# Two hT tiles, a new split of PSUM for batch 0 and a newly searched order in an attention-then-MoE kernel

## The chip, the cores and the metric

One core of a Trainium2 chip. A time is the device time of one execution in microseconds (us); what is compared are medians of several executions and ratios of fast runs. A run counts as slow when it is over 1.5% above the fastest run of the same kernel; with one core there is no second die to compare with. The profile is of one execution, and its span, from the first to the last instruction, is some 1.6 us shorter than that execution's time.

## The reference

Eight batches. In each, eight heads of 576 rows and 64 columns go through a linear attention (k^T v, then q times that), a norm over the 64 columns, and then as one sequence of 576 rows of 512 through one expert, chosen for the whole batch by the mean of its rows.

```python
def _attn_ref(q, k, v, g_norm):                       # (8, 8, 576, 64)
    kv = np.einsum('bhsd,bhse->bhde', k, v)
    out = np.einsum('bhsd,bhde->bhse', q, kv)
    rms = np.sqrt(np.mean(out * out, axis=-1, keepdims=True) + 1e-06)
    return out / rms * g_norm

def _moe_ref(x, w_gate, w1, w2):                      # x (8, 576, 512), w1 (8, 512, 1024), w2 (8, 1024, 512)
    logits = x.mean(axis=1) @ w_gate
    e_idx = np.argmax(logits, axis=1)
    ...                                               # gate_w: softmax probability of the chosen expert
    h = np.maximum(x[mask] @ w1[e], 0.0)
    out[mask] = gate_w[mask, None, None] * (h @ w2[e])
```

With the inputs the batches choose experts 4, 4, 7, 6, 5, 1, 3, 1. So batch 1 needs no new weights (batch 0 has them), and batch 7 has those of batch 5.

## The kernel before

The kernel is written as small steps, and one string gives the order in which all of them are emitted. Each engine's program then has its own instructions in that order. A token is batch, step, index, and an x where the step's copy or eviction goes to the other of VectorE and ScalarE. The steps that matter here:

- L0, L1, L2: load q, k or v of a batch (GpSimd issues it, 576 KB each; the load casts f32 to f16).
- T, K, O, M, X: transposes of q; k^T v; q times it; the mean of squares (ones times the squares); the normed xT.
- G0 to G3: the gate; G1 reads the chosen expert into a register.
- W0, W1: fetch the expert's first and second weights ("W1 of batch b" is bW0, "W2 of batch b" is bW1; 1024 KB each as f16).
- m0 to m7: the eight units of mm1 (x times W1, into hT); m8 and m9 to m16: mm2 (hT times W2).
- D: dummy matmuls that keep TensorE busy; P: batch 0's own PSUM tiles are given back.

## Time and profile before

| | before |
|---|---|
| time, median of 3 runs | 195.28 us (195.17 to 196.23) |
| span of the profiled run | 191.9 us |
| first matmul of mm1 starts | 30.84 us |
| TensorE idle from 40 to 160 us | 1.65 us |
| last eviction starts, then the end | 187.49 us, 4.4 us |

The main readings (busy shares, slices, windows, chain) are shown in the prediction below.

The timeline of TensorE ahead of mm1 (start us, us, engine, line, operation, out and in, shapes):

```profile
24.59 1.90 PE L149 MATMUL ps_a<-kvb,ones 128*128 128x512 f16 x7
...
26.74 0.95 PE L192 MATMUL ps_a<-vt,kt 96*64 96x64 f16 x48
...
30.84 2.06 PE L348 MATMUL ps_m<-xT,W 128*128 128x288 f16 x8
```

Seven dummies of 512 columns take 1.90 us, 271 ns each; K of batch 1 takes 0.95 us.

### The profile page before, as it was taken

The page shows a single profiled execution, that of the slowest core. Times are in us where ns is not written, and L with a number is a line of the kernel's source. Part 1 is how long each engine was busy: PE and PEld are TensorE (multiplying, and loading weights), DVE is VectorE, ACT ScalarE, POOL GpSimd, SP SyncE. Part 2 cuts the span into 40 slices and gives each one's busy share as a digit, 9 for nine tenths or more (in the row PEclk, how much of TensorE's full clock was granted, in tenths as well). Part 3 has the DMA queues.
Part 4 walks back from the last instruction along what each step waited for, and adds up shares of the span by engine and source line. Part 5 has one row for each costly group of instructions (what it writes and reads, how often), then busy time and mean ns, then how long its engine had stood idle before and what let it go on. Part 6 is the DMA issues. An engine that isn't in the chain of part 4 may idle for free.

```text
span 191.9 us, 4365 instructions
## 1 busy us (share of the span) xinstructions
PE 172.1 (90%) x1691; PEld 113.8 (59%) x1691; DVE 111.2 (58%) x289; ACT 106.6 (56%) x168; POOL 49.9 (26%) x64
## 2 busy tenths in 40 slices
PE   0296687998999999999999999999999999999990
PEld 0153255784668755886478746857686568457540
DVE  2437373867979695775666785697665482431010
ACT  2146105676878757876666656665357656216521
POOL 7770098008223150016117030311022103000000
PEclk9999997999999999999999999999999999999999
DMA  5999999999999999999999999999999898162044
GB/s 157 187 201 206 201 199 186 205 205 204 218 236 246 218 208 215 256 242 204 212 262 236 205 219 243 262 194 177 243 255 181 150 171 195 29 164 59 0 130 116
DMA packets 37031, 36.92 MB, mean 192 GB/s; under 512 B 2706, under 2 KB 30354, under 8 KB 37010
## 3 DMA queue, kind: packets, MB, share of 16 engines
q0 software_dynamic: 29328, 26.30, 86.4%
q1 hardware_dynamic: 7474, 10.05, 18.3%
q10 hardware_dynamic: 208, 0.29, 0.5%
q8 instruction: 13, 0.21, 0.4%
q14 instruction: 8, 0.07, 0.1%
HBM read 61.88 MB, written 9.44 MB: 372 GB/s over the span
## 4 chain that ended last, share of the span: by engine, by line
PE 71%; DMA 16%; DVE 5%; ACT 3%; issue 2%; POOL 2%; POOLq 0%
PE ps_m L348 32%; PE ps_m L387 25%; DMA qt<-in_q_dram 7%; DMA W<-in_moe_w_dram 5%; PE ps_a L224 4%; DMA kt<-in_k_dram 4%; PE ps_a L207 3%; PE ps_a L160 3%; PE ps_m L375 3%; DVE o L179 2%; ACT sq L212 2%; PE ps_a L192 2%; DVE qr L174 1%; POOL qt L103 1%; DVE W L311 1%
## 5 line engine op out<-in xcount | busy, mean ns | idle before, releaser
L348 PE MATMUL ps_m<-xT,W 128*128 128x288 f16 x512 | 69.5, 289 | 0.1
L387 PE MATMUL ps_m<-W,hT 128*128 128x512 f16 x256 | 60.7, 379 | 0.2 <-DMA W<-in_moe_w_dram 0.2
L348 PEld LDWEIGHTS <-W 128*128 128x128 f16 x512 | 50.0, 99 | 13.3 <-issue 0.2
L355 ACT ACTIVATE hT<-ps_m 128x576 f16<-128x576 f32 x51 | 33.2, 652 | 21.0 <-PE ps_m L348 20.7
L387 PEld LDWEIGHTS <-hT 128*128 128x128 f16 x256 | 24.2, 98 | 24.8 <-DMA W<-in_moe_w_dram 0.8
L322 POOL DMA_DIRECT2D W<-in_moe_w_dram x20 | 12.5, 627 | 74.3 <-DVE W L311 23.6
L359 ACT ACTIVATE ot<-ps_m,gates 128x512 f32<-128x512 f32 (+1 forms) x26 | 17.0, 656 | 18.5 <-PE ps_m L387 12.2
L228 ACT ACTIVATE rs<-ps_a,epsc 128x576 f32<-128x576 f32 x28 | 20.5, 741 | 7.5 <-PE ps_a L224 7.0
L237 DVE SCALAR_TENSOR_TENSOR xT<-o,gcol,rs 128x576 f16<-128x576 f32 x28 | 22.4, 812 | 3.6 <-ACT rs L228 3.6
L212 ACT ACTIVATE sq<-ps_a 128x576 f16<-128x576 f32 x28 | 17.9, 648 | 10.9 <-PE ps_a L207 10.8
L179 DVE COPY o<-ps_a 128x576 f32<-128x576 f32 x20 | 15.0, 757 | 14.0 <-ACT sq L212 13.8
L275 POOL TENSOR_TENSOR lg<-base,dl 128x8 f32<-128x8 f32 x8 | 14.2, 1771 | 29.3 <-DVE src L294 16.8
L311 DVE COPY W<-W 128x2048 f16 (+1 forms) x28 | 19.3, 696 | 2.6 <-DVE src L294 0.8
L361 DVE TENSOR_SCALAR ot<-ps_m,gates 128x512 f32<-128x512 f32 (+1 forms) x14 | 9.4, 674 | 17.8 <-PE ps_m L387 15.9
L179 ACT COPY qT<-ps_a 128x576 f16<-128x576 f16 x15 | 9.5, 636 | 10.7 <-PE ps_a L160 10.7
L352 DVE TENSOR_SCALAR hT<-ps_m 128x576 f16<-128x576 f32 x13 | 9.8, 755 | 8.1 <-PE ps_m L348 8.1
L192 PEld LDWEIGHTS <-kt 96*64 96x64 f16 x384 | 7.5, 116 | 9.9 <-ACT kt L179 6.0
L224 PE MATMUL ps_a<-sq,ones 128*128 128x288 f16 x56 | 11.1, 286 | 2.1 <-DVE o L179 2.0
L207 PE MATMUL ps_a<-qT,kvb 128*128 128x288 f16 x56 | 11.6, 291 | 0.8 <-DVE o L179 0.5
L224 PEld LDWEIGHTS <-ones 128*128 128x128 f16 x64 | 6.0, 99 | 7.9 <-issue 3.2
L160 PEld LDWEIGHTS <-qr 96*128 96x128 f16 x144 | 8.9, 100 | 2.9 <-issue 0.4
L160 PE MATMUL ps_a<-ident,qr 96*128 96x96 f16 x144 | 10.4, 209 | 0.2 <-DVE dl L269 0.2
(75 smaller groups left out, 135.1 us busy)
## 6 DMA issues: line engine op xcount, KB each, us to landing
W<-in_moe_w_dram POOLq DMA_DIRECT2D x14, 1024.0 KB, 14.2
out_dram<-ot SPq DMA_DIRECT2D x24, 192.0 KB, 5.8
qt<-in_q_dram POOLq DMA_DIRECT2D x7, 576.0 KB, 14.4
kt<-in_k_dram POOLq DMA_DIRECT2D x7, 576.0 KB, 10.0
vt<-in_v_dram POOLq DMA_DIRECT2D x7, 576.0 KB, 16.1
out_dram<-ot SPq DMA_DIRECT2D x40, 64.0 KB, 5.6
out_dram<-ot SPq DMA_DIRECT2D x16, 128.0 KB, 5.2
W<-in_moe_w_dram POOLq DMA_DIRECT2D x4, 256.0 KB
```

What stands on the lines that cost most here:

```text
L160: nc.tensor.transpose(pt[:, 0, j * R:(j + 1) * R], s["qr"][0:R, c, j], ident[0:R, 0:R])
L179: nc.scalar.copy(out, in_) if x else nc.vector.tensor_copy(out, in_)
L207: nc.tensor.matmul(po[:, i, 0:HS], kvb[:, b % 2, c, :], s["qT"][:, c, i * HS:(i + 1) * HS], start=True, stop=True)
L212: nc.scalar.activation(part(s["sq", c], h), po, AF.Square)
L224: nc.tensor.matmul(pm[:, i if h is None else 0, 0:HS], ones, s["sq", c][:, i * HS:(i + 1) * HS], start=True, stop=True)
L228: nc.scalar.activation(part(s["rs", c], h), pm[:, 0:2 if h is None else 1, 0:HS], AF.Abs_reciprocal_sqrt, bias=epsc)
L237: nc.vector.scalar_tensor_tensor(out=part(s["xT"][:, c, :], h), in0=s["o", c, h], scalar=gcol, in1=part(s["rs", c], h), op0=ALU.mult, op1= ...
L311: nc.vector.tensor_copy(W[:, own, h * n:(h + 1) * n], W[:, ds(sv, 1), h * n:(h + 1) * n].rearrange("p o c f -> p (o c) f"))
L348: nc.tensor.matmul(ph[:, i, 0:HS], w1[:, c, fb * P:(fb + 1) * P], s["xT"][:, c, i * HS:(i + 1) * HS], start=(c == 0), stop=(c == 3))
L355: nc.scalar.activation(two(s["hT"][:, fb, :]), ph[:, :, 0:HS], AF.Relu)
L359: nc.scalar.activation(out, in_, AF.Copy, scale=gates[:, b:b + 1])
L387: nc.tensor.matmul(po[:, 0, :], s["hT"][:, fc, t * P:(t + 1) * P], w2[:, fc, :], start=(fc == 0), stop=(fc == 7))
```

## The change

Its intent: with two hT tiles the mm1 of a batch can run ahead of mm2 of the batch in front, so that TensorE always has something to do; batch 0 gets three pairs of PSUM banks for O and two single banks for everything else, with M done by halves; and the order is searched anew for this.

```diff
-    hp = ctx.enter_context(tc.tile_pool(name="hp", bufs=1))
+    hp = ctx.enter_context(tc.tile_pool(name="hp", bufs=2))
@@ s_qt, s_kv, s_row, D: batch 0's tags t and kv become two single banks in common
-        p32 = psum("t", 1, 1) if first[0] else psum("a")
+        p32 = psum("s", 2, 1) if first[0] else psum("a")
@@ s_o
-        po = (psum("p", 1) if h == 1 else psum("m")) if first[0] else psum("a")
+        po = psum("m", 3) if first[0] else psum("a")
@@ s_m: in batch 0 one half of the columns after the other
+        for hs in ((0,), (1,)) if first[0] and h is None else ((0, 1) if h is None else (h,),):
+            pm = psum("s", 2, 1) if first[0] else psum("a")
+            ...
@@ the copy of qT (token C) now takes the token's x, and so can go to ScalarE
-            s_tc(b, c)
+            s_tc(b, c, x)
```

And the order (… marks cuts):

```diff
 start of mm1
-… 0X31x 0G1x 0W0x 2L1x 0P0x 0D1 1T1 1T2 1T3 0D1 0D1 0D1 0D1 0D1 0W1 0D1 2Q0x 0D1 0G2x 1K0 …
+… 0X31x 0G1x 1T0 0P0x 1T2 1T3 0W0x 1T1 0D1 2L1 0D1 0D1 2Q0 0D1 0D1 0W1x 3L0x 0G2x 1K0x …
 W2 of batch 2, loads of batches 5 and 6
-… 5L2x 5L1x … 2W0 1m6 1m4x 3M2x 1m3 3M1x 4K0x 2W1 1m11 4T1 6L0x …
+… 5L1 6L0 … 2W0 4K0x … 5L2 … 5T1x 2W1 1m10 … 6L2 6Q0 6L1x …
 W2 of batch 4, loads of batch 7
-… 4W0 … 7L1 … 4W1x 5X3x … 3m16x 7L2 4m0x …
+… 4W0x … 7L0x 3m3 6O0 7L1 … 5M3 7L2x 3m15x 6O1 3m11 4W1 …
 W2 of batch 5
-… 5W0x 6X0x 4m3 6O3 5G3 5W1x 4m6 …
+… 5W0 4m5 … 5G3x 4m9 4m10 … 4m11 6G1x 5W1 4m12x …
```

The dummies are 11 in place of 17: six in batch 0 in place of nine, and five after the release of batch 0's PSUM in place of eight.

## The prediction

> **What bounds the kernel now.** I read the page's busy shares and slices first, to see which engine is full and when. The slices are 4.8 us each, in tenths.
>
> ```profile
> span 191.9 us, 4365 instructions
> PE 172.1 (90%) x1691; PEld 113.8 (59%) x1691; DVE 111.2 (58%) x289; ACT 106.6 (56%) x168; POOL 49.9 (26%) x64
> PE   0296687998999999999999999999999999999990
> PEclk9999997999999999999999999999999999999999
> DMA  5999999999999999999999999999999898162044
> ```
>
> The reader is to see three stretches: some 31 us in which TensorE is not full, a long one in which it is, and an end of a few us. The DMA engines are full from the second slice until about 155 us, so TensorE and the DMA queue are bounds side by side. VectorE and ScalarE have 40% to spare.
>
> Next the windows by microsecond and over the long stretch; columns are the busy time of TensorE, its weight loads, VectorE, ScalarE and GpSimd, then granted clock, DMA share and GB/s.
>
> ```profile
> 29.00:30.00 1.00, 0.47 (x3) 0.19 (x2) 0.22 (x1) 0.91 (x3) 1.00 (x1) 1.00 1.33 171
> 30.00:31.00 1.00, 0.41 (x3) 0.29 (x3) 1.00 (x2) 0.29 (x1) 1.00 (x2) 0.95 1.39 193
> 31.00:32.00 1.00, 1.00 (x6) 0.63 (x5) 0.44 (x3) 0.74 (x1) 1.00 (x2) 0.50 1.43 186
> 33.00:34.00 1.00, 1.00 (x9) 0.73 (x8) 0.46 (x1) 0.69 (x2) 0.00 (x0) 0.50 1.30 191
> 34.00:35.00 1.00, 1.00 (x9) 0.72 (x8) 0.42 (x1) 0.55 (x1) 0.00 (x0) 0.85 1.32 204
> ...
> 34.00:187.50 153.50, 151.73 (x1426) 101.86 (x1424) 95.32 (x237) 94.95 (x151) 30.79 (x34) 1.00 1.04 195
> ```
>
> From 34 to 187.5 us TensorE idles 153.50 - 151.73 = 1.77 us in all. At 31 to 34 us it is busy at half clock.
>
> Then the chain of waits and the timeline around the first mm1 of batch 0, for what sets the 31 us. In the chain the columns are start, length and what.
>
> ```profile
> 11.61 14.27 DMA qt<-in_q_dram
> ...
> 30.59 0.40 PE ps_a L224 x2
> 31.00 1.90 PE ps_m L348 x8
> ...
> 42.46 0.40 ACT hT L355
> ...
> 127.33 10.08 DMA W<-in_moe_w_dram
> ...
> 187.49 0.47 ACT ot L359
> ```
>
> ```profile
> 24.30 3.01 POOL L322 DMA_DIRECT2D W<-in_moe_w_dram  x4 [11.16 <-DVE qT L179]
> 27.30 0.79 POOL L103 DMA_DIRECT2D kt<-in_k_dram  x1
> ```
>
> The first mm1 (its first matmul starts at 30.84 us in the timeline) needs the first quarter of W1 of batch 0. Its four loads are issued from 24.30 us on, behind q and v of batch 2. Landings: q of batch 2 at 11.61 + 14.27 = 25.88. For v of batch 2 the tile's view gives a longest landing of 16.9 us, and it was issued at 12.37, so 29.27. For k of batch 2 the issue at 27.30 has a landing of 9.9 us, so 37.2. Between 29.27 and 37.2 lie the 1.05 MB of W1 and the 0.59 MB of k: 1.64 MB in 7.9 us, 207 GB/s, which is what the DMA row moves anyway. So my estimate is that the W1 quarters landed near 30.5, 31.8, 33.1 and 34.3 us. The first weight load of mm1 was at 30.72. The chain ascribes the start to q of batch 2, its copies and O and M of batch 1, but W1 itself came at the same moment: both end within 0.3 us of each other.
>
> [...] 0.50 in the middle windows, and 0.95, 0.50 three times, 0.85 over 30 to 35 us (one row is cut above) give 0.1 + 3 + 0.3 = 3.4 us at half clock, right after a stretch in which TensorE was a bit over half busy. [...] eight matmuls of 288 columns take 0.98 us in the chain, 122.5 ns each, and four of 512 columns 0.86 us, 216 ns each. [...]
>
> **The accounts of the span before.** 191.9 = 30.84 to the first mm1 + 156.65 from there to the last eviction at 187.49 + 4.4 of eviction and output. The 156.65 are 1.77 of idle, 3.4 us at half clock which cost 1.7, and the rest, 153.2, of work that is also in the new kernel. By kind (from the chain's lengths): 64 mm1 units of 0.98 = 62.7; 64 mm2 units of 0.865 = 55.4; eight small ones of 0.99 = 7.9; some 27 O and 28 M of 0.245 = 13.5; 25 transposed pairs of 0.26 = 6.5; six K of 0.88 and seven gates of 0.12 = 6.1. That gives 152.2, close to 153.2.
>
> **The change part by part.**
> (a) Two hT tiles. No wait in the profile is on hT being free: in the old order every mm2 of a batch stands before the first mm1 of the next. So this part by itself removes nothing; it lets the order put an mm1 of the next batch where TensorE now waits. In the new order the first mm1 of batch 1 stands before the first mm2 of batch 0. W1 of batch 1 needs no load then: batches 0 and 1 choose the same expert (calculated from the reference), so it is a copy on VectorE, two of 0.69. Where could it fill? In the ten us from 40 to 50 TensorE idles 0.85 us, at the seam from mm1 to mm2 of batch 0; from 90 to 100 us 0.51; in the rest 0.4. I expect the new order to take away about half of the 1.77, 0.9 us. It cannot be more than 1.77.
> (b) Batch 0 with six banks for O and two for the rest. O needn't wait for a bank any more; T, K, M and the dummy matmuls share two single banks instead. M by halves makes two ScalarE instructions of 0.50 out of one of 0.74, three times: 3 x 0.26 = 0.8 us more on ScalarE. Three copies of qT go to ScalarE (0.64 in place of 0.46). The new order also no longer puts a transposition of batch 1 (which waited for its q until 17.2 us) ahead of O of the last pair. I put the gate of batch 0 between 2 us earlier and 0.5 us later than now. None of that is on the path: W1's loads could be issued as late as 29.27 us, when the queue runs out ahead of them, and they are issued at 24.3. The queue before them is the same in the new order: q and v of batch 2 still ahead. Worth 0.
> (c) The start of mm1. The new order has three O of batch 1 ahead of it, the third of which waits for a bank as M did before (a copy by VectorE that ends at 30.55), then mm1 at 30.8. At most 0.3 us is left before W1 lands. I take 0.1.
> (d) Dummy matmuls: 11 in place of 17. The six that fall away lie in TensorE's idle time: 0 on the path. But they held the clock, and this is the uncertain term. A half-clock window costs 1.7 us when it falls on mm1.
> (e) The end: again a unit of 256 columns, one eviction and one output, 4.4 us.
> Sum: 30.84 - 0.1 + 153.2 + 0.9 + 1.7 + 4.4 = 190.9 us of span, 1.0 us less than before.
>
> **From span to time.** The profiled run took 193.51 us with its span of 191.9; the three timed ones 195.17 to 196.23. The 1.7 us between 193.51 and 195.2 have the size of one more half-clock window in those runs; this is a guess, as they left no trace. I leave this surplus of 3.4 us over the span as it is: 190.9 + 3.4 = 194.3. That the new start may have fewer slow windows (one in five, 1.7 us less, so 0.3 on average) brings me to 194.0.
>
> **The rivals.**
> 1. The DMA queue takes over. For it: DMA full to 155 us; W1 of batch 5 landed at 137.41 and its mm1 began at 137.46; k of batch 5 landed 18.5 us after its issue at 53.37, at 71.9, and W1 of batch 2, next in the queue, can hardly land before 77 to 78, where its mm1 began at 78.77. A TensorE that comes sooner meets the same landings. Against it: the last W2 is needed at 163.47 and the queue was through by about 157, so a good order of loads has slack. If it holds, the gain is 0 to 0.5: 195.
> 2. The clock decides. With no slow window on mm1 and the idle time gone, the time falls to 194.3 - 1.7 - 0.9 = 191.7, with a surplus window gone too to 190. With one more, it is 196. For a loss speak the six dummies less[...].
> 3. The batch-0 part matters after all, and mm1 starts 2 us sooner: 192. Against it stands the landing of W1 behind v of batch 2, which would have to change places.
> 4. Two shared banks make batch 0 so slow that the gate comes after 29 us: mm1 late by a few us, 197. I estimate nearly 5 us of slack, so this is unlikely.
>
> **Range and chances.** Centre 194.0, from 192.0 (one slow window less and some more idle filled) to 195.6 (the queue takes over, or a further slow window). Faster by over 2% means under 191.4: it needs the clock and the idle time together, 11%. Slower by over 2% means above 199.2, which no rival reaches: 2%. Within 2%: 87%.
>
> **What would show it.** Right: the first mm1 at 30.5 to 31 us; W's four loads issued at 22 to 25 us with no earlier mm1; idle of TensorE between 34 us and the end at 0.5 to 1.3 us; work from the first mm1 to the last eviction some 155 to 156 us; as many dummies fewer as said; an end of 4.4 us. Wrong: a first mm1 well before 30 us (then the queue wasn't the bound), waits of weight loads for W of over 1 us (rival 1), a slow window added or gone in the granted clock (rival 2), or a wait for the two shared banks that moves the gate beyond 27 us (rival 4).

## More of the kernel before

```python
hp = ctx.enter_context(tc.tile_pool(name="hp", bufs=1))     # hT, [128, 8, 576] f16
...
def load_qkv(b, parts, which=None, only=range(3)):
    ...
            nc.gpsimd.dma_start(t[0:R, hs], src[b, hs].rearrange("h (p j) d -> p h (j d)", j=NJ))
...
def s_w(b, i):                                              # token bW0 or bW1
    own = b % NW                                            # three slots for each of W1 and W2
    W = (W1, W2)[i]
    cond = None
    if b > 0:
        ...                                                 # sv: slot of a batch in front that may have this expert
        for h in range(2):
            n = W.shape[2] // 2
            nc.vector.tensor_copy(
                W[:, own, h * n:(h + 1) * n],
                W[:, ds(sv, 1), h * n:(h + 1) * n].rearrange("p o c f -> p (o c) f"))
        for e in evs[max(0, b - 2):b]:
            c = evs[b] != e
            cond = c if cond is None else s_logical_and(cond, c)
    ...
        nc.gpsimd.dma_start(W[:, own, :, fs], (moe_w1, moe_w2)[i][ds(ev, 1), :, fs]
                            .rearrange("o (c p) f -> p (o c) f", p=P), cond=cond)
...
def m_1(b, fb, x=False):
    if fb == 0:
        s["hT"] = hp.tile([P, 8, S], F16, tag="hT", name="hT")
...
def warm(t, n):                                             # token D
    for _ in range(n):
        nc.tensor.matmul(t[:, 0, :], ones, kvb[:, 1], start=True, stop=True)
...
for tok in ORDER.split():
    emit(tok)
```

Two things in this code carry the argument. VectorE always copies a neighbour's weights into the new slot, and only then may the load, which happens if the expert is a new one, overwrite them. And the loads of q, k and v and of the weights are all issued by GpSimd, one after another in the order of the string.

What TensorE waits for (engine, line and what for: us in total, times, longest us):

```profile
PE ps_m L387 <- DMA W<-in_moe_w_dram: 0.2, 1, 0.2
```

So mm2 (line 387) practically never waits for its weights.

The timeline of GpSimd, with what ended its idle time in brackets:

```profile
52.34 0.77 POOL L103 DMA_DIRECT2D vt<-in_v_dram  x1 [0.61 <-issue]
53.37 0.78 POOL L103 DMA_DIRECT2D kt<-in_k_dram  x1 [0.26 <-issue]
...
67.08 0.81 POOL L322 DMA_DIRECT2D W<-in_moe_w_dram  x1 [4.05 <-DVE W L311]
...
70.21 0.89 POOL L322 DMA_DIRECT2D W<-in_moe_w_dram  x1 [2.32 <-DVE W L311]
```

The two last are W1 and W2 of batch 2; each was let go by VectorE's copy into its slot (line 311). v and k of batch 5 were issued 14 us ahead of them. The windows (busy TensorE, its weight loads, VectorE, ScalarE, GpSimd; granted clock; DMA share; GB/s):

```profile
45.00:55.00 10.00, 9.61 (x119) 5.65 (x117) 8.74 (x21) 7.85 (x13) 5.15 (x8) 1.00 1.29 219
70.00:80.00 10.00, 10.00 (x123) 6.35 (x122) 7.73 (x20) 7.29 (x13) 1.67 (x2) 1.00 1.15 227
```

The queue of loads moves 219 and 227 GB/s in both stretches.

## The result and the profile after

| | before | after |
|---|---|---|
| time, median of 4 runs side by side | 195.22 us (193.23 to 196.23) | 203.24 us (201.52 to 205.02) |
| ratio of the fast runs | | 1.0417 (95%: 1.0284 to 1.0549) |
| span of the profiled run | 191.9 us | 202.0 us |

A ratio is the mean time of one kernel's fast runs over that of the other's of the same rounds, so it isn't quite the ratio of the medians quoted. The kernel is slower by 4%; to a loss of over 2% the prediction gave a chance of 2%. The four runs of the new kernel had spans from 199.9 to 203.4 us, so the profiled one is no outlier.

The page of the kernel after, slices of 5.05 us:

```profile
span 202.0 us, 4359 instructions
...
PE   2488797999999899989999999959994999999990
...
PEclk9999999999999999999999999999999699999998
```

TensorE has lost its long full stretch: two dips, to 5 and to 4 tenths, at about 131 and 152 us, with a slice at lower clock right behind the second. What it waits for there:

```profile
PE ps_m L387 <- DMA W<-in_moe_w_dram: 5.3, 2, 2.9
...
PE ps_a L192 <- DMA vt<-in_v_dram: 0.8, 1, 0.8
```

The first row is the one that stood at 0.2 before. The first of its two waits ends here:

```profile
134.26 1.90 PE L387 MATMUL ps_m<-W,hT 128*128 128x512 f16 x8 [2.36 <-DMA W<-in_moe_w_dram]
```

And the chain of waits has the two loads that end them, what stands between them, and the work behind the second:

```profile
116.82 17.39 DMA W<-in_moe_w_dram
...
139.24 0.13 PE ps_a L281 x2
...
140.19 0.71 DVE W L311
...
142.23 13.04 DMA W<-in_moe_w_dram
...
155.32 7.04 PE ps_m L387 x24
```

They are W2 of batch 4, issued at 116.82 us and landed at 134.21, and W2 of batch 5, issued at 142.23 and landed at 155.27. The second wait hangs on the first: W2 of batch 5 is copied (140.19) only behind the gate of batch 6, whose matmul (139.24) stands behind mm2 of batch 4, which had to wait for W2 of batch 4 until 134.26. After the second, 24 matmuls of 512 columns take 7.04 us; at the 216 ns that one takes at full clock in the trace before they would take 5.18. The windows of one us show why:

```profile
154.00:155.00 1.00, 0.00 (x0) 0.00 (x0) 0.00 (x0) 0.00 (x0) 0.00 (x0) 1.00 1.15 219
...
157.00:158.00 1.00, 1.00 (x3) 0.30 (x2) 0.18 (x1) 0.00 (x0) 0.00 (x0) 0.50 0.80 150
```

TensorE stood from 152.38 to 155.32 us, and at 154 to 155 us no engine computes, only the DMA engines work. From 156.51 us on the clock is at half, for 3.4 us. So the wait is paid for twice, 2.94 us of idle and 1.86 at half clock.

The start, in the timeline of TensorE of the kernel after:

```profile
23.31 1.93 PE L164 MATMUL ps_a<-ident,qt 96*64 96x96 f16 x36 [0.61 <-DVE row L431]
25.18 2.53 PE L149 MATMUL ps_a<-kvb,ones 128*128 128x512 f16 x5
...
28.16 1.50 PE L192 MATMUL ps_a<-vt,kt 96*64 96x64 f16 x48
...
33.28 2.12 PE L348 MATMUL ps_m<-xT,W 128*128 128x288 f16 x8
```

Five dummies take 2.53 us, 506 ns each in place of 271, and K of batch 1 takes 1.50 us in place of 0.95. That is half clock, and it lasts from the first matmul until some 37 us, although the row PEclk shows nines there: the record of the clock has no entry ahead of 37.05 us (ahead of 13.83 in the kernel before). Whether the start runs so differs between executions: of the profiles below that have this same start, four have K of batch 1 at 1.50 us and two (W2 of batch 2 directly behind its W1; the loads of the fourth group moved together) at 0.95. So part of a late start is chance, and two profiles are best compared with this in mind.

The accounts, in the terms of the prediction (work is what remains):

| part of the span | before | after | difference |
|---|---|---|---|
| until the first mm1 | 30.84 | 33.28 | +2.44 |
| TensorE idle from there to the last eviction | 1.77 | 6.82 | +5.05 |
| half clock from there on | 1.66 | 3.68 | +2.02 |
| work | 153.2 | 153.1 | −0.1 |
| from the last eviction to the end | 4.41 | 5.15 | +0.74 |
| span | 191.9 | 202.0 | +10.1 |

The half clock of the kernel after is 1.82 at the start (in the chain the first mm1 takes 1.92 in place of 0.98, four M 0.96 in place of 0.48, part of the second mm1 1.38 in place of 0.98) and 7.04 − 5.18 = 1.86 behind the wait for W2 of batch 5. The work is the same, as predicted. Everything else is waiting and clock. The 0.74 at the end lie beside four output transfers issued for the last two units (7m8 and 6m8x, both of the small form) in place of two; no run took that apart.

**Where the loads went.** The same two windows as before, now of the kernel after:

```profile
45.00:55.00 10.00, 9.97 (x82) 6.84 (x81) 7.25 (x18) 8.10 (x14) 4.15 (x5) 1.00 1.24 180
70.00:80.00 10.00, 10.00 (x94) 5.72 (x90) 7.86 (x21) 7.21 (x13) 2.14 (x3) 1.00 1.05 176
```

The queue moved 180 and 176 GB/s in place of 219 and 227. In these 20 us that is 10 us × 39 GB/s + 10 us × 51 GB/s = 0.9 MB less, nearly a whole weight load. And this is the timeline of GpSimd at that place:

```profile
70.58 0.81 POOL L322 DMA_DIRECT2D W<-in_moe_w_dram  x1 [3.96 <-DVE W L311]
71.39 0.79 POOL L103 DMA_DIRECT2D vt<-in_v_dram  x1
...
79.45 0.89 POOL L322 DMA_DIRECT2D W<-in_moe_w_dram  x1 [7.27 <-DVE W L311]
```

W1 of batch 2 is issued at 70.58 in place of 67.08, v of batch 5, whose token now stands behind that of W1, only after it (71.39 in place of 52.34), and W2 of batch 2 at 79.45 in place of 70.21, after GpSimd has stood 7.27 us for VectorE's copy. In the trace v goes out right behind the weight load of 70.58 that waited 3.96 us, and no load is issued while GpSimd stands at a weight load, 3.96 and 7.27 us here; so a weight load that waits for its copy holds back the q, k and v behind it. The queue ran thin, and W2 of batches 4 and 5, issued at 116.82 and 142.23 us in place of 113.67 and 130.54, took 17.39 and 13.04 us to land; in the trace before the longest landing of a weight load is 15.3.

### The profile page after: what moved, and what is told of

It is laid out like the page before. It is cut to its first block, busy times and chain, and to the rows that moved or that the text cites. A ratio compares the mean times of both kernels' runs of the same rounds, so it can differ in the third digit from the quotient of the medians.

```text
span 202.0 us, 4359 instructions
## 1 busy us (share of the span) xinstructions
PE 178.8 (89%) x1685; PEld 116.9 (58%) x1685; DVE 111.9 (55%) x290; ACT 104.8 (52%) x170; POOL 49.9 (25%) x64
## 4 chain that ended last, share of the span: by engine, by line
PE 58%; DMA 26%; issue 6%; DVE 4%; ACT 3%; POOL 1%; POOLq 0%; DVEq 0%; ACTq 0%
PE ps_m L387 20%; PE ps_m L348 20%; DMA W<-in_moe_w_dram 15%; DMA vt<-in_v_dram 11%; PE ps_a L207 2%; PE ps_m L375 2%; PE ps_a L192 2%; PE ps_a L226 2%; PE ps_a L160 2%; DVE W L311 1%; PE ps_a L149 1%; ACT sq L212 1%; PE ps_s L226 1%; ACT rs L228 1%; PE ps_s L164 1%
## 5 line engine op out<-in xcount | busy, mean ns | idle before, releaser
L348 PE MATMUL ps_m<-xT,W 128*128 128x288 f16 x512 | 70.6, 289 | 0.0
L387 PE MATMUL ps_m<-W,hT 128*128 128x512 f16 x256 | 62.2, 387 | 5.3 <-DMA W<-in_moe_w_dram 5.3
L387 PEld LDWEIGHTS <-hT 128*128 128x128 f16 x256 | 25.1, 100 | 31.2 <-DMA W<-in_moe_w_dram 5.8
L322 POOL DMA_DIRECT2D W<-in_moe_w_dram x20 | 13.0, 653 | 117.5 <-DMA W<-in_moe_w_dram 25.2
L359 ACT ACTIVATE ot<-ps_m,gates 128x512 f32<-128x512 f32 (+1 forms) x22 | 14.3, 651 | 31.4 <-PE ps_m L387 18.9
L361 DVE TENSOR_SCALAR ot<-ps_m,gates 128x512 f32<-128x512 f32 (+1 forms) x18 | 12.4, 690 | 21.2 <-PE ps_m L387 19.0
L179 DVE COPY o<-ps_a 128x576 f32<-128x576 f32 x18 | 13.5, 757 | 15.2 <-ACT sq L212 15.1
L226 PE MATMUL ps_a<-sq,ones 128*128 128x288 f16 x56 | 11.8, 297 | 0.6 <-DVE o L179 0.6
L192 PEld LDWEIGHTS <-kt 96*64 96x64 f16 x384 | 8.5, 123 | 3.9 <-issue 3.8
L207 PEld LDWEIGHTS <-kvb 128*128 128x128 f16 x64 | 6.4, 104 | 7.0 <-issue 2.5
## 6 DMA issues: line engine op xcount, KB each, us to landing
out_dram<-ot SPq DMA_DIRECT2D x24, 192.0 KB, 2.6
```

The costliest lines, as they stand in the source:

```text
L207: nc.tensor.matmul(po[:, i, 0:HS], kvb[:, b % 2, c, :], s["qT"][:, c, i * HS:(i + 1) * HS], start=True, stop=True)
L226: nc.tensor.matmul(pm[:, n, 0:HS], ones, s["sq", c][:, i * HS:(i + 1) * HS], start=True, stop=True)
L348: nc.tensor.matmul(ph[:, i, 0:HS], w1[:, c, fb * P:(fb + 1) * P], s["xT"][:, c, i * HS:(i + 1) * HS], start=(c == 0), stop=(c == 3))
L359: nc.scalar.activation(out, in_, AF.Copy, scale=gates[:, b:b + 1])
L387: nc.tensor.matmul(po[:, 0, :], s["hT"][:, fc, t * P:(t + 1) * P], w2[:, fc, :], start=(fc == 0), stop=(fc == 7))
```

## The experiments

Where an edit is given as a change of order, only the tokens moved and their neighbours are shown. "New order" is that of the kernel after. All runs gave right results. Each group ran on another chip, with the kernel before beside it (the kernel after was not run again); its medians in the five groups were 196.73, 195.98, 195.05, 195.95 and 194.67 us. About half of its runs in these groups fell in the slow state, nearly all of these at a recorded clock of 0.95 to 0.98, the fast ones at 0.97 to 1.00; so medians of different groups compare poorly, and the ratios of fast runs are the better measure.

### First group: the parts alone

Theory: the loss comes from the later order, waits for W2. Rivals: the late start makes the waits; the second hT tile costs something itself.

**Two hT tiles alone**, in the old kernel:

```diff
-    hp = ctx.enter_context(tc.tile_pool(name="hp", bufs=1))
+    hp = ctx.enter_context(tc.tile_pool(name="hp", bufs=2))
```

> The old kernel with two hT tiles and nothing else changed. Theory: the second tile alone does nothing, as no wait of the old kernel is on hT: 194.5 to 196, ratio 0.995 to 1.005. Rival (the second tile costs something by itself, or lets an eviction go earlier): a ratio beyond that.

Measured: 195.28 us in 20 runs, ratio 0.9987 (0.994 to 1.0035). The tile is neutral, as the prediction said.

**The new start with the old later order**: two hT tiles, the new batch 0 with its PSUM split and order up to P, then the old order.

```diff
 (new order up to) … 0G1x 1T0 0P0x
+0W0x 2L1x (then the old order from there, without what is done already)
```

> The changed kernel's batch 0 (its banks, halves of M, its order up to the release of the first pool) with two hT tiles, and the old order from there on. Theory (the loss is in two parts, a cold start of some 2.5 us plus 1.7 us of half clock on the first mm1, and later waits for W2): only the start is lost, first mm1 at 32.5 to 33.5 us, no wait for W2 over 1 us, 197 to 199 us. Rival 1 (only the later order loses): 195 to 196. Rival 2 (the late start makes the later waits, by pushing loads back): 201 or more, with W2 waits of 2 us or more.

Measured: 198.56 us (194.2 to 199.16), three of four runs slow, the profiled one among them (span 197.5). K waited for v that landed late (longest 2.3 us), the first mm1 came at 35.85 us; no wait for W2. One fast run gives no ratio, so this is inconclusive as to size; it shows only that the waits for W2 don't come with the new start.

**The old start with the new later order**: old batch 0, two hT tiles, the new order after it.

> The old kernel's batch 0 and start, with two hT tiles and the new order from the release of the first pool on. Theory: first mm1 near 31 us, but the two waits for W2 (2.4 and 2.9 us) are there still, 199 to 201 us. Rival 1 (only the later order loses): 202 to 204. Rival 2 (the late start makes the waits): 194 to 196 without W2 waits.

Measured: 201.81 us (198.47 to 203.15), ratio 1.0247 (0.99 to 1.06, only two fast runs). The first mm1 started at 32.24 us, a microsecond ahead of the kernel after, and the waits for W2 were still 4.2 us (this is a slow run, so its sizes don't count, but the waits are those of the kernel after). So the later order carries them by itself, and the rival that a late start makes them falls. The ratio is too wide to say more.

**More dummies, for the clock** (new order):

```diff
-0R2x 0D1 0R1x 2L0x 0R0x 0D1 0T0x …
+0R2x 0D6 0R1x 2L0x 0R0x 0D6 0T0x …      (two dummies for one in batch 0, three for one after P)
```

> The changed kernel with 6 dummy matmuls where it has 1 at the first two places, and 2 or 3 where it has 1 at the other nine. Theory (the start is late because TensorE stays at half clock until 33 us): transposes of 0.45 us in place of 0.69 from about 10 us on, first mm1 at 30.5 to 31.5 us, 3 to 4 us less than the changed kernel: 199 to 200.5. Rival (the start is late because of the two shared banks and the order, whatever the clock): first mm1 at 33 or later, 203 or more.

Measured: 199.69 us, ratio 1.0257 (1.0063 to 1.0451). The number fits, the mechanism doesn't: the clock was full by 7.6 us but half again from about 12 to 22 us, after a stretch of 6 to 10 us in which TensorE was 33% busy. And the fifteen dummies behind P, now at full clock, took 3.4 us ahead of K of batch 1. The first mm1 started at 33.45, no sooner. The gain lies later: waits for W2 of 3.1 us in place of 5.3, and no half clock behind them. Dummies are work on the path once something stands behind them.

### Second group: the loads, and the clock

**The loads of batch 7 and W2 of batches 4 and 5 put back** towards their old places (new order):

```diff
-… 6O0 7L1 … 5M3 7L2x … 3m11 4W1 … 3m8x 7K0 … 4m10 7O0x … 6G1x 5W1 …
+… 6O0 … 5M3 … 3m11 4W1 7L1 7L2x … 3m8x … 5G3x 5W1 4m9 4m10 7K0 7O0x … 6G1x …
```

> The changed kernel with four tokens of the order moved: k and v of batch 7 are loaded after W2 of batch 4 and not before it; K of batch 7 stands right before its first O; the copy and load of W2 of batch 5 stand before the first mm2 of batch 4 and not after most of them. Theory (W2 of batch 4 is late because the loads of batch 7 stand ahead of it in the queue[...]): W2 of batch 4 lands near 128 us in place of 134, the 2.4 us and 2.9 us waits of TensorE go, and the half-clock window after the second too: 5 to 7 us less than the changed kernel, 196 to 198. Rival (the copies from slot to slot set the pace, each W2 being copied only when the one in front has landed): the waits stay within 1 us of what they were, 202 or more.

Measured: 203.88 us, ratio 1.0494 (1.035 to 1.063). The theory as it stood falls: the waits for W2 went, and others came. From the chain of waits of this run:

```profile
119.36 17.45 DMA vt<-in_v_dram
```

v of batch 7 now stands where W2 of batch 4 stood, with the same 17 us to landing. K waits for v in two places, 3.3 us in sum, 2.8 of them the longest; the waits for W2 are down to 0.6. So the queue is behind by that time, and the load that stands last in it is the late one.

**VectorE's copies of the weights left out** for batches 2 to 6 (new order; right with these inputs alone, where each of those batches loads its own):

```diff
-            for h in range(2):
+            for h in range(0 if 2 <= b <= 6 else 2):
```

> The changed kernel without the copies of W from slot to slot for batches 2 to 6, whose experts are new each, so that the result stays right on this data: a load of W then waits for no load of the batch in front. Theory of the queue: W2 of batch 4 lands as late as it did, as k and v of batch 7 are still ahead of it, and W2 of batch 5 is still issued after the gate of batch 6; less than 2 us gained, 201 to 204. Rival (the copies set the pace): both waits gone, 196 to 198.

Measured: 196.9 us (195.85 to 197.13), ratio 1.0146 (1.006 to 1.023): most of the loss is gone, with not one token moved. From the windows and the chain:

```profile
70.00:80.00 10.00, 10.00 (x93) 5.73 (x88) 6.33 (x18) 7.21 (x13) 0.00 (x0) 1.00 1.21 219
```

```profile
104.15 27.76 DMA W<-in_moe_w_dram
```

The queue is full again at 70 to 80 us, 219 GB/s; at 45 to 55 us, where only batch 1's copy (left in) and the order matter, it stays at 180. W2 of batch 4 is issued 12.7 us sooner, though it lands only 2.3 us sooner (131.91 against 134.21), as it stands behind other loads. TensorE was 10.00 us busy in that window in both kernels, so it isn't that VectorE's time had held TensorE up there: what the copies held up is the issue of loads. W2 waits fell to 1.4 us, and no half-clock stretch followed.

**The old kernel without its nine dummies in batch 0**:

```diff
-… 0C1 0D1 0O1x … 0C2x 0D1 0D1 0O2x … 2L2x 0D1 0D1 0D1 0X2 0M31 0D1 0X30 0D1 0D1 0X31x …
+… 0C1 0O1x … 0C2x 0O2x … 2L2x 0X2 0M31 0X30 0X31x …
```

> The old kernel without its nine dummy matmuls in batch 0 (the eight after it stay). Theory (these hold the clock up from 14 us on): transposes of 0.69 us in place of 0.45 until at least 25 us, the first mm1 at 32.5 to 34 in place of 30.84, 197 to 199 us. Rival (the clock rises without them, it is the two shared banks that keep TensorE idle in the new batch 0): the first mm1 within 0.7 us of the old one, 195 to 196.

Measured: 196.11 us, ratio 1.0042 (0.9993 to 1.0092). The first mm1 started at 33.02 us in its profile, as late as in the kernel after, with K of batch 1 at half clock (1.50 us). That profile is of a slow run, and its span of 194.7 us is 2.8 above that of the kernel before: there the late start was paid for in full. The fast runs (9 of 20), which the ratio compares, left no trace, so how late they started is not known. The start half of the expectation came true, then, and the time half (197 to 199) did not. The recorded clock was 0.98 or more in each of the 20 runs, against down to 0.95 in those of the kernel before; but the record lacks the start.

**The kernel after without the five dummies behind P**:

```diff
-… 1T1 0D1 2L1 0D1 0D1 2Q0 0D1 0D1 0W1x …
+… 1T1 2L1 2Q0 0W1x …
```

> The changed kernel without the five dummy matmuls behind the release of the first pool. Theory (at half clock they take 2.5 us and stand in line ahead of K of batch 1, on the way to the first mm1): K of batch 1 at 25.5 to 26.5 us, first mm1 at 30.5 to 31.5 in place of 33.3, the later waits stay: about 1.5 to 2.5 us less than the changed kernel, 200.5 to 202. Rival 1 (a later wait swallows it, as W2 comes when it comes): first mm1 as said, but 202.5 to 204. Rival 2 (without them the clock stays low for longer): first mm1 early, but half clock for another 3.4 us or more.

Measured: 198.77 us, ratio 1.0241 (1.014 to 1.034), against 1.0417 with them: 4.5 us by the medians, more than expected. The first mm1 started at 31.14 us, 2.1 us sooner, with K of batch 1 at half clock as in the kernel after. The waits for W2 were 4.0 us in place of 5.3, and no half-clock stretch came behind the second, which is another 1.9 us. So the dummies at half speed were on the path.

### Third group: one copy moved, all copies moved, and the cross of copies and order

**W2 of batch 2 directly behind its W1** (new order):

```diff
-… 2W0 4K0x … 5T1x 2W1 1m10 …
+… 2W0 2W1 4K0x … 5T1x 1m10 …
```

> The changed kernel with one token moved: the copy and load of W2 of batch 2 directly behind those of its W1, some 9 us earlier. Theory (the DMA queue runs half empty from 70 to 80 us because W2 is copied late, and what it doesn't move then is missing at W2 of batch 4): 205 GB/s or more from 70 to 80 us in place of 176, W2 of batch 4 lands 1.5 to 2.5 us earlier, the two waits for W2 sum to 3 us or less in place of 5.3: 199.5 to 201.5. Rival (the gain without the copies was VectorE's time, 14 us of it): waits and time as in the changed kernel, 202 to 204.

Measured: 208.36 us, ratio 1.0721. Worse, and the theory in this form falls. The timeline says why:

```profile
89.09 1.49 PE L191 MATMUL ps_a<-vt,kt 96*64 96x64 f16 x48 [5.28 <-DMA vt<-in_v_dram]
```

v of batch 5 now stands behind both weights of batch 2 in the queue; K of batch 5 waits 5.28 us for it, and half clock follows.

**All weight loads sooner, no dummies behind P** (new order; W2 of batches 2 to 5 moved up, K of batch 7 later):

```diff
+… 2W0 2W1 … 3W1 6L2 … 4W1 7L0x … 5G3x 5W1 4m9 4m10 7K0 7O0x …
```

> The changed kernel without the five dummy matmuls, with W2 of batches 2 to 5 copied and loaded earlier (behind W1 of batch 2; ahead of v of batch 6; ahead of q of batch 7; ahead of mm2 of batch 4) and K of batch 7 right before its first O. Theory (start and queue are the whole loss): first mm1 at 31 us, waits for W2 under 1.5 us in sum, 193.5 to 196, even with the old kernel. Rival (the bytes ahead of mm2 of batch 4 are the bound, and another load is late in place of W2, as v of batch 7 was): a wait for v of batch 7 of 2 us or more, 198 to 200.

Measured: 212.53 us, ratio 1.09. Worse still: v of batch 5 late by 5.2 us, then k of a later one by 2.4, and M waited 3.6 us for a copy that stood on VectorE behind a late q. TensorE was idle 14.5 us between 40 and 160 us. Moving only the weights pushes q, k and v back.

**Copies left out and no dummies behind P** (new order):

> The changed kernel without the copies of W for batches 2 to 6 (right on this data only) and without the five dummy matmuls. Theory (the two losses are apart and add up): the first mm1 at 31 us, 192.5 to 195. Rival (TensorE that comes earlier waits the longer for the queue, so that they overlap): 195.5 to 197, with waits for W2 of 3 us or more.

Measured: 196.38 us, ratio 1.0124 (1.0067 to 1.0182), hardly better than without the copies alone (1.0146). The first mm1 started at 31.23 us, and W2 was waited for 1.0 us, not the 3 us or more of the rival. What the traces show of an overlap is that either edit alone already takes away the half clock behind the second wait (1.9 us) and part of the waits (5.3 us, 4.0 without the dummies, 1.4 without the copies). That a start 2 us sooner meets the same landings is not shown.

**Copies left out in the old order**:

> The old kernel without the copies of W for batches 2 to 6 (right on this data only). Theory (the old order copies W2 3 us after W1 and keeps the queue full, so the copies cost nothing there): within 1 us of the old kernel of the same rounds. Rival (the copies cost by VectorE's time in any order): 3 us or more less.

Measured: 194.74 us, ratio 0.9968 (0.9925 to 1.001). In the old order leaving out the same copies wins 0.3%, which can't be told from nothing; in the new one it wins 2.7% (1.0417 against 1.0146). The copies are in both kernels. What the new order changed is what stands behind them.

### Fourth group: loads and weights moved together

**k of batch 4, v and k of batch 5 and W2 of batch 2 sooner, q of batch 6 behind them** (new order):

```diff
-… 4L0x 2O1x … 5L0 2O3 … 5L1 6L0 … 2W0 4K0x … 5L2 … 2W1 …      (and 4L1x further back)
+… 4L0x 4L1x 2O1x … 5L0 5L2 5L1 2O3 … 2W0 2W1 6L0 4K0x …
```

> The changed kernel with five tokens moved so that the loads up to 80 us are issued as in the old order: k of batch 4 behind its q, v and k of batch 5 ahead of W2 of batch 1, W2 of batch 2 directly behind its W1, q of batch 6 after both. Theory (GpSimd issues loads in order and stands at loads of W that wait for copies, so that the queue runs thin at 45 to 55 and 70 to 80 us, and all later loads shift by that): 200 GB/s or more in both stretches, no wait for v of batch 5, waits for W2 of 3.5 us or less in sum, 199 to 201. Rival (the new order asks for W2 too early whatever the loads): waits for W2 of 5 us or more, 202 to 204; a wait of 3 us or more elsewhere would also count for it.

Measured: 201.8 us, ratio 1.0301 (1.018 to 1.042). No wait for v of batch 5, but still 4.0 us for W2 of batches 4 and 5. The profiled run was a slow one, with the start late by v of batch 0; in it the queue moved 201 and 168 GB/s in the two windows, where 200 or more was expected in both.

**The same, and the later loads as in the second group** (W2 of batch 5 behind 5G3, v of batch 7 behind W2 of batch 4, K of batch 7 later):

```diff
+… 4W1 7L2x … 5G3x 5W1 4m9 4m10 7K0 7O0x …      (on top of the edit above)
```

> As the run with the early loads moved, and as well v of batch 7 loaded behind W2 of batch 4, K of batch 7 right before its first O, and W2 of batch 5 copied and loaded ahead of the first mm2 of batch 4, all as in the old order. Theory: waits for W2 of 1.5 us or less in sum, none for v of batch 7 over 1 us, 196.5 to 198.5. Rival: another load takes the wait's place, 200 or more.

Measured: 197.24 us in 20 runs, ratio 1.0077 (1.0033 to 1.0121). No wait for W2 is left in its profile, and the queue moves 222 GB/s at 45 to 55 us and again 213 at 70 to 80:

```profile
70.00:80.00 10.00, 10.00 (x86) 6.14 (x85) 6.57 (x22) 7.79 (x13) 0.83 (x2) 1.00 1.13 213
```

Of the 4.2%, 3.4 are back, with all copies and all dummies in place; by the medians of all runs it is the same (197.24 over 195.95, against 203.24 over 195.22). So most of the loss was in where loads and copies stood. The profile alone would say too much:

```profile
27.51 0.95 PE L191 MATMUL ps_a<-vt,kt 96*64 96x64 f16 x48
```

K of batch 1 ran at full clock here, and the first mm1 began at 31.66 us in place of 33.28, though the order up to there is that of the kernel after. With the 1.82 us of half clock on the first mm1s that is 3.4 of the 7.3 us between the two spans, and not the edit's. It may also be what parts the 11 fast runs (up to 197.4 us) from the 9 slow ones (198.4 to 201.0), 7 of which have a recorded clock above 0.99; they left no trace, so this is not shown. Three smaller waits are new in its timeline:

```profile
69.69 0.42 PE L206 MATMUL ps_a<-qT,kvb 128*128 128x288 f16 x2 [1.08 <-DVE kvb L196]
...
133.49 0.42 PE L206 MATMUL ps_a<-qT,kvb 128*128 128x288 f16 x2 [1.36 <-DVE kvb L196]
```

At 69.69 O waits for the copy of K's result, which stands on VectorE behind two weight copies; at 133.49 K of batch 7 is right in front of O and its copy takes time; the third is 0.99 at 91.6 us, an eviction behind a rearrangement that waits for q.

**The same without the five dummies behind P**:

> As the last one, without the five dummy matmuls behind the release of the first pool. Theory (start and loads are the whole loss): the first mm1 at 31 us, 194 to 196, even with the old kernel. Rival (the earlier TensorE meets the same queue): as without this, 197 or more.

Measured: 197.42 us, ratio 1.0168 (1.013 to 1.0206). No further gain, and the interval is above the one with dummies. 17 of its 20 runs counted as fast, against 11 of 20 with dummies, and the medians differ by 0.2 us. Its profile is of a slow run: v of batch 0 landed late, and the first mm1 came at 33.12, so the start at 31 us that was expected can't be checked there.

**The old kernel without any of its 17 dummies**:

> The old kernel without any of its 17 dummy matmuls. Theory (W1 of batch 0 sets the first mm1, the dummies only stand in line ahead of K of batch 1; the clock is slow until mm1 has run for some 3 us, at the cost of 1.7 us): first mm1 at 30.5 to 31.5 us, half clock on the first mm1s, within 1.5 us of the old kernel. Rival (the dummies pay): 2 us or more slower.

Measured: 194.78 us in 20 runs, median 1.2 us below that of the kernel before (195.95), but ratio 1.008 (1.0044 to 1.0116). Both are true: 19 of its 20 runs are fast ones at a recorded clock of 0.99 or more, while of 55 runs of the kernel before 25 were fast and 30 slow. The dummies make the best case better by 0.8% and the middle one no better.

### Fifth group: the three new waits mended

**The loads sooner, with 2W1 and 6L0 behind 4K0x, 6Q0 later, K of batch 7 one unit ahead of its O**:

```diff
-… 2W0 2W1 6L0 4K0x … 6L2 6Q0 6L1x … 4X3x … 4m9 4m10 7K0 7O0x 4m15x …
+… 2W0 4K0x 2W1 6L0 … 6L2 6L1x … 4X3x 6Q0 … 4m9 7K0 4m10 4m15x 7O0x …
```

> As the run with early and late loads moved, with its three new waits mended (1.1, 1.0 and 1.4 us in its trace): W2 of batch 2 copied behind the copies of K of batch 4, the rearrangement of q of batch 6 later, K of batch 7 one mm2 earlier and its first O one later. Theory (what is left of the loss are these three waits): 2 to 3 us less than that run, 194 to 195.5, even with the old kernel of the same rounds (ratio 0.99 to 1.005). Rival (other waits take their place): a ratio of 1.005 to 1.02.

Measured: 198.84 us in 6 runs, ratio 1.0233 (1.017 to 1.0296). In the trace the three waits are gone, and two smaller ones for loads have come (1.1 us for W1 of batch 4 at 117, 1.2 for v of batch 7 at 134); idle from 40 to 160 us fell from 4.10 to 2.97. But the first mm1 started at 33.60 us in this run, against 31.66, with K of batch 1 at half clock; the order of the start is the same in both. The ratio is worse than without the mends (1.0077), so the theory that these waits are what is left of the loss falls.

**The same without the five dummies behind P**:

> The last one without the five dummy matmuls behind the release of the first pool. Theory (the start sets the end once the loads come in time): 1 to 2 us less than the last one, 192.5 to 194.5, faster than the old kernel by 0.5 to 1%. Rival (as in the run pair before, the dummies make no difference once the loads are moved, since TensorE meets the same queue, or runs its first mm1s at half clock): within 0.7 us of the last one.

Measured: 195.98 us in 6 runs, all fast, ratio 1.0128 (1.0083 to 1.0174). First mm1 at 30.89 us, idle 2.95, span 193.4. The ratio is lower than that of the same without the mends (1.0168), but the intervals overlap, so a gain by the mends is not shown. Against the profiled run of the kernel before, that span is 1.5 us longer: 0.05 to the first mm1, 0.7 at the end (5.15 against 4.41), and 0.7 in between (157.36 against 156.65).

### The runs together

Idle is that of TensorE between 40 and 160 us in the profiled run. K of batch 1 tells the clock at the start: 0.95 us is full, 1.50 half.

| kernel | ratio | K of batch 1, us | first mm1, us | idle, us | span, us |
|---|---|---|---|---|---|
| before | 1 | 0.95 | 30.84 | 1.65 | 191.9 |
| after | 1.0417 | 1.50 | 33.28 | 6.79 | 202.0 |
| after, without 5 dummies | 1.0241 | 1.49 | 31.14 | 5.49 | 197.1 |
| after, without copies | 1.0146 | 1.50 | 33.35 | 2.07 | 195.5 |
| after, without both | 1.0124 | 1.49 | 31.23 | 1.70 | 193.6 |
| after, loads sooner | 1.0077 | 0.95 | 31.66 | 4.10 | 194.7 |
| after, loads sooner, mended | 1.0233 | 1.50 | 33.60 | 2.97 | 197.6 |
| the same without 5 dummies | 1.0128 | 1.49 | 30.89 | 2.95 | 193.4 |

Of all runs none with the new order beats the kernel before, which remains the one to use.

## Why the prediction was wrong

The predicted time was 194.0 us (192.0 to 195.6), the measured 203.24. Point by point:

**What was right.** Two hT tiles by themselves remove no wait (ratio 0.9987). The work from the first mm1 on is unchanged (153.1 us against the predicted 153.2). Step (b): the gate of batch 0 came within its range: W1 was issued at 24.08 us against 24.30 before, so banks and halves were worth 0. The guess that the timed runs have more half-clock stretches than the profiled one is borne out: runs of the kernel before with a recorded clock of 0.98 to 1.00 had spans of 190.8 to 193.6 us (two had 194.1 and 194.2), those with 0.95 to 0.977 had 193.8 to 198.2. (The prediction's tally of work by kind adds up to 152.1, not 152.2; nothing hangs on it.)

**The step that failed most: (a),** "I expect the new order to take away about half of the 1.77, 0.9 us. It cannot be more than 1.77." Idle time became 6.82 us. The bound was on the gain only; nothing in the step bounded a loss. The working looked at the order at the first seam and at the first loads, and not at where the later loads and weight fetches stand between the other tokens, although the change said "order searched anew". Put side by side as in the diff above, the order shows W2 of batch 5 moved behind the gate of batch 6, W2 of batch 4 behind all loads of batch 7, and v of batch 5 behind W1 of batch 2. The trace before showed that GpSimd stood for VectorE's copies (4.05 and 2.32 us in the timeline shown above), so what stands behind a weight fetch is issued when a copy is done.

**Rival 1 had the mechanism and the wrong sign of its size.** It named the queue and wrote "If it holds, the gain is 0 to 0.5: 195." It took landings as fixed, so that a TensorE that comes sooner only waits for them. But the order sets the issues too. (That these loads land in order of issue is what the trace before shows for three of them: q, v and k of batch 2 at 25.88, 29.27 and 37.2 us.) That an earlier issue behind other loads gains nothing, on which step (b) rests too, was the author's estimate; without the copies W2 of batch 4 was issued 12.7 us sooner and landed 2.3 us sooner. The later issues of the new order left the queue thin, 180 and 176 GB/s in place of 219 and 227. The waits for W2 were 5.3 us and the half clock behind them 1.9. Leaving out the copies (1.0146), or moving loads and weights together (1.0077), takes most of the loss back, which shows that the issue of the loads caused most of it. That it wasn't VectorE's time, which is freed too when the copies go, is what the old order speaks for: there the same copies cost 0.3%, which can't be told from nothing. Moving only some (1.0494, 1.0721, 1.09) handed the wait to another load.

**Step (d), "0 on the path".** The six dummies fewer were counted, and those that stay were taken to lie in idle time. The five behind P took 2.53 us at half clock right in front of K of batch 1, and the first mm1 came 2.44 us later; without them it came at 31.14. The six that fell away were not free either: the old kernel without its nine in batch 0 also starts at half clock (K of batch 1 at 1.50 us in place of 0.95), with its first mm1 at 33.02 in the one profile there is. The prediction named the clock as its uncertain term, but sized it only as 1.7 us where it falls on mm1, and not on the way there. Step (c), 0.1 us sooner, fell with it. How much of the 2.44 us is chance is open: with the same start at full clock the first mm1 came at 31.66.

**Step (e),** an end of 4.4 us with one output, was off by 0.7 us: the new order ends with two small units and four output transfers, 5.15 us.

**"Slower by over 2% means above 199.2, which no rival reaches".** No rival joined a thin queue, a slow start and the half clock that follows a wait. They don't seem to add up: without dummies the time falls 4.5 us, without copies 6.3, without both 6.9 (medians of different groups against 203.24), not 10.8; both edits take away the half clock behind the second wait.

**What stays open.** The best versions of the new order are still 0.8 to 1.3% behind the old one in fast runs. In one profile 0.7 us of that lie at the end and 0.7 in waits; no run settled whether the end alone can be mended. What a late start costs in fast runs of the old order is open, as its one profile with a start 2 us late is of a slow run (with two hT tiles alone, a fast run began mm1 1.27 us late but at full clock, and its span was 0.8 us longer). And why the clock at the start is full in some executions and half in others with the same start is not settled.

## What to carry to other kernels

When an order is searched anew, list for the old and the new one where each load is issued relative to the work that needs it, and which waits stand in front of it on the issuing engine; a bound on the idle time that can be won says nothing on what can be lost. Where one engine issues all loads in order and some of them wait for a copy, see which loads stand behind each of these: here v of batch 5, put behind W1 of batch 2, was issued at 71.39 us in place of 52.34, and moving one load back only handed the wait to the next (1.0494, 1.0721). Dummy matmuls are not free once real work stands behind them: five at half clock, 2.53 us, made the first mm1 2.1 us later. And a profile is one execution: see which clock it started with before its parts are set against another's.
